# The first token loads of a 2048-token attention-plus-MLP block: two transfers of two token blocks each, one issued by SyncE and one by ScalarE

## The chip, the cores and the metric

The kernel runs on one core of a Trainium2 chip. The metric is the device time of one execution in microseconds (us). TensorE is called PE here, VectorE DVE, ScalarE ACT, GpSimd POOL and SyncE SP, as in the profile. PEld is PE's weight load.

## The reference

One pre-norm transformer block over 2048 tokens of width 640, in bfloat16: a layer norm, a linear-memory ("infini") attention with 32 heads of 20 in four segments of 512 tokens, a residual, a second layer norm, a 640-1728-640 MLP with SiLU, and a residual.

```python
q, k, v = x @ wq, x @ wk, x @ wv             # x = layernorm(A_x); 32 heads, 4 segments of 512 tokens
for s in range(4):
    p = softmax(q[s] @ k[s].T * scale + mask)            # causal inside the segment
    a_mem = (phi(q[s]) @ M) / (phi(q[s]) @ z + 1e-6)     # memory of earlier segments
    o[s] = g * a_mem + (1 - g) * (p @ v[s])              # g = sigmoid(beta), per head
    M += phi(k[s]).T @ v[s];  z += sum(phi(k[s]))
h = A_x + o @ wo
out = h + silu(layernorm(h) @ w1) @ w2
```

## The kernel before

The tokens are worked on in 16 blocks of 128 (one block is 128 partitions of 640 elements, 160 KB) and in four segments of four blocks. A segment runs through layer norm, projections, scores with exp, values, memory, output projection, second norm and MLP. The segments overlap in time.

Nothing decides an order at run time. Each step is a named task, and the text `ORDER` lists all tasks in one sequence; every engine executes its own tasks in that sequence, each instruction waiting on semaphores for what it reads. A number behind a name gives the buffer that the task takes (`x0:0` puts token block 0 into slot 0 of `x_tok`), and a letter behind a slash gives the engine where there is a choice (`A` is ACT, `D` DVE, `G` POOL). Without a letter a task goes to the first engine in its list.

The names at the start of the sequence that matter here:

- `x0`, `x1`, `x2`: loads of token blocks from `A_x` into `x_tok` (line 598, `load_x(first block, number of blocks, ..., engines)`). Before, x0 is block 0, x1 is block 1, x2 is blocks 2 and 3 in one transfer, all issued by SP. Blocks 4 to 7 (`x4`) and 8 to 11 (`x8`) come later.
- `w_q0`, `w_q1`, `w_k0`, `w_k1`, `w_wv`, `beta`: the loads of the query, key and value weights and of beta (lines 601 and 609), from SP, directly behind the token loads.
- `warm`: ACT loads its function table and runs one activation on zeros (line 618).
- `n1_st0` to `n1_st3`: mean and variance of a block. Blocks 0, 1 and 3 are done by DVE (lines 785, 788, 791), block 2 by ACT (lines 778, 780, 801).
- `n1_rs*`: reciprocal standard deviation, on POOL (line 808; 811 and 813 for block 2). `n1_ap*`: the normalised block, on DVE (line 819).
- `n1_tp*`: PE's transposition of the normalised block (line 828, five matmuls against the identity). `n1_te*`: its copy from PSUM, on ACT (line 837) or DVE (line 838).
- `fill*`: matmuls on zeros, which keep PE occupied at the start (line 637).
- `pr000x`, `pr001x`, `pr001y`, `pr000y`: the first query and key projections (line 752), from the raw weights, for blocks 0 and 1 (x) and blocks 2 and 3 (y). They are PE's first work with a result that lasts.

On DVE the sequence is statistics of block 0, statistics of block 1, normalise block 0, statistics of block 3, normalise blocks 1, 3 and 2. On PE it is transpositions of blocks 0, 1 and 3, the first part of `pr000x`, the transposition of block 2, and the rest.

Of the kernel before, what the change touches and what calls it, by code (L numbers as in the profile page):

```python
# [11 lines left out]
PE, AC, DV, PO, SP = "pe", "act", "dve", "pool", "sp"  # L12
# [368 lines left out]

ORDER = """
x0:0 zpad:0 iota fill25:7 vpad0 x1:3 sel halfc mq0 x2:5,6 warm:0 w_q0:0 epsc w_q1 n1_st0:1 w_k0:0 w_k1 w_wv:0 n1_st1:0
n1_rs0 beta n1_ap0:0 n1_rs1 fill4:5 n1_st2:5,1 n1_st3:4 fill8:5 mq1 n1_tp0:2 n1_ap1:2 n1_rs3 n1_te0:1 n1_tp1:0 n1_rs2
fill2:5 n1_ap3:3 n1_mn2 n1_te1 n1_tp3:6 n1_ap2 re_wq1/A:0 pr000x.0:3 n1_te3/D x4:2,10,11,1 n1_tp2:4 pr000x.1
x8:9,8,4,7 n1_te2 pr001x.0:1 qe000x/D:0 re_wk1/G pr001x.1 re_wk2/A pr001y.0:2 re_wk4/G pr001y.1 qe001x pr000y.0:6
# [97 lines left out]
def build(nc, es, A_x, A_wq, A_wk, A_wv, A_wo, A_beta, B_x, B_w1, B_w2, out):  # L484
# [52 lines left out]
    zpad = sb("zpad", [128, 256], BF16)  # L537
# [37 lines left out]
    def dma(name, reads, writes, fn, prio, bw, kind="plain", lane=None, engs=(SP,)):  # L575
        ln = T.lane(name) if lane is None else lane

        def emit(eng):
            T.add(eng, lambda e: fn(e), reads=R(*reads), writes=R(*writes), lane=ln)
        cost = {"tr": 1.31, "plain": 0.47, "sb": 0.72, "fix": 0.47}[kind]  # L580
        t = G.task(name, {e: cost for e in engs}, emit, reads, writes, prio, mode=kind, bw=bw)
        return t
# [12 lines left out]
    def load_x(b0, n, prio, bw=2.1, kind="plain", engs=(SP, AC)):  # L595
        s0 = b0 % 12
        dma(f"x{b0}", [(W["wk"], ["p"])] if b0 >= 4 else [], [(X[b], [0]) for b in range(b0, b0 + n)],
            lambda e: e.dma_start(out=x_tok[:, s0:s0 + n, :], in_=xv[:, b0:b0 + n, :]), prio, bw, kind, engs=engs)

    def load_w(k, dst, src, prio, bw, wr, kind="plain", engs=(SP, AC)):  # L600
        dma("w_" + k, [(W["wk"], ["p"])] if kind == "plain" else [], wr, lambda e: e.dma_start(out=dst, in_=src), prio, bw, kind, engs=engs)

    cw = lambda w: w.rearrange("(c p) e -> p c e", p=128)
    load_x(0, 1, -100, 2.30, "fix", (SP,))
    load_x(1, 1, -99, 2.33, "fix", (SP,))
    load_w("wv", wv_sb[:, :, :], cw(A_wv), -98, 4.96, [(W["wv"], [0])], "fix", (SP,))
    load_x(2, 2, -97, 4.79, "fix", (SP,))
    dma("beta", [], [(C, ["beta_bc"])],
        lambda e: e.dma_start(out=beta_bc[:, :],
                              in_=A_beta.rearrange("(o n) -> o n", o=1).to_broadcast([128, H])), -92, 4.65, "fix")  # L610
# [50 lines left out]
    sel = ident[:, :].rearrange("p (r e) -> p r e", e=32)[:, :, 0:VS]  # L661
# [695 lines left out]
def bass_sequential_preLN__memory_aug_infini_attn__dense_activation_silu__prompt_kernel(  # L1357
    nc, A_x, A_wq, A_wk, A_wv, A_wo, A_beta, B_x, B_w1, B_w2, out
):
    es = ExitStack()  # L1360
    with es:
        T, finals, _ = build(nc, es, A_x, A_wq, A_wk, A_wv, A_wo, A_beta, B_x, B_w1, B_w2, out)
        with nc.Block() as block:
            T.emit(nc, block, es, final_waits=finals)
# [28 lines left out]
```

## Time and profile before

| | |
|---|---|
| median of 3 runs | 292.54 us (292.24 to 292.88) |
| the profiled execution | 292.8 us, its span 291.1 us |
| PE busy, PEld busy | 283.0 us (97%), 156.9 us (54%) |
| DVE, ACT, POOL busy | 208.7, 224.7, 138.1 us |
| granted TensorE clock | 1.0 throughout |
| DMA queue of the kernel's transfers (q1) | 48688 packets, 24.19 MB |
| HBM | 10.41 MB read, 2.62 MB written |

The span is the time from the first to the last recorded event on the core; the rest of an execution's time lies around it. "The chain of waits" is the work that ended last, followed back step by step to what released each step; listed in order of time it gives a start, a duration and the engine with the source line. A timeline row gives the start, the duration, the engine, the line and the operation, then what was written and read, the number of instructions, and in brackets the idle time ahead of the first with what ended it. SPq is SP issuing transfers.

### The profile page before, as it was taken

The page shows a single profiled execution, that of the slowest core. Times are in us where ns is not written, and L with a number is a line of the kernel's source. Part 1 is how long each engine was busy: PE and PEld are TensorE (multiplying, and loading weights), DVE is VectorE, ACT ScalarE, POOL GpSimd, SP SyncE. Part 2 cuts the span into 40 slices and gives each one's busy share as a digit, 9 for nine tenths or more (in the row PEclk, how much of TensorE's full clock was granted, in tenths as well). Part 3 has the DMA queues.
Part 4 walks back from the last instruction along what each step waited for, and adds up shares of the span by engine and source line. Part 5 has one row for each costly group of instructions (what it writes and reads, how often), then busy time and mean ns, then how long its engine had stood idle before and what let it go on. Part 6 is the DMA issues. An engine that isn't in the chain of part 4 may idle for free.

```text
span 291.1 us, 10526 instructions
## 1 busy us (share of the span) xinstructions
PE 283.0 (97%) x4587; PEld 156.9 (54%) x4587; DVE 208.7 (72%) x435; ACT 224.7 (77%) x286; POOL 138.1 (47%) x275
## 2 busy tenths in 40 slices
PE   8999989999999999999999999999999999999995
PEld 6544434445544446566643554655565557754674
DVE  5599889769998679369979972776676659436513
ACT  4999999999999999999689989999849750024300
POOL 4686668608670766609516761638435531200000
PEclk9999999999999999999999999999999999999999
DMA  7916439854565333343551327512110031340004
GB/s 207 350 57 125 85 65 303 116 55 79 121 110 126 67 86 101 47 76 60 101 183 17 66 43 102 78 19 49 25 25 2 2 69 26 75 131 0 3 5 160
DMA packets 48734, 24.86 MB, mean 85 GB/s; under 512 B 38896, under 2 KB 47472, under 8 KB 48688
## 3 DMA queue, kind: packets, MB, share of 16 engines
q1 hardware_dynamic: 48688, 24.19, 37.9%
q8 instruction: 36, 0.59, 0.9%
q14 instruction: 10, 0.08, 0.1%
HBM read 10.41 MB, written 2.62 MB: 45 GB/s over the span
## 4 chain that ended last, share of the span: by engine, by line
PE 79%; ACT 13%; DVE 4%; DMA 2%; POOL 1%; issue 1%; SPq 0%; DVEq 0%; ACTq 0%
PE ps_all L565 41%; PE ps_all L566 23%; ACT PT L1024 9%; PE ps_all L1003 7%; PE ps_all L1059 5%; ACT PT L1020 2%; DMA x_tok<-in_A_x_dram 2%; PE ps_all L1130 1%; PE ps_all L752 1%; PE ps_all L1268 1%; ACT ex L930 1%; POOL PT L1036 1%; DVE om L1149 1%; ACT oTs L1073 1%; PE ps_all L1189 1%
## 5 line engine op out<-in xcount | busy, mean ns | idle before, releaser
L1024 ACT ACTIVATE PT<-ps_all 128x1024 bf16<-128x1024 f32 x122 | 117.9, 1030 | 7.9 <-PE ps_all L1003 6.8
L1036 POOL TENSOR_SCALAR_AFFINE_SELECT PT<-PT 128x512 bf16<-128x512 bf16 x128 | 81.6, 666 | 71.6 <-ACT PT L1024 59.5
L1281 ACT ACTIVATE th<-ps_all 128x512 f32<-128x512 f32 (+1 forms) x56 | 31.5, 591 | 30.1 <-PE ps_all L565 22.5
L1287 DVE SCALAR_TENSOR_TENSOR sT<-th,ps_all 128x512 bf16<-128x512 f32 (+1 forms) x56 | 36.2, 661 | 16.8 <-ACT th L1281 16.5
L1020 ACT ACTIVATE PT<-ps_all 128x2048 bf16<-128x2048 f32 x19 | 35.7, 1878 | 3.5 <-PE ps_all L1003 3.4
L565 PE MATMUL ps_all<-w_sb,sT 128*128 128x320 bf16 x252 | 37.0, 299 | 0.0
L565 PE MATMUL ps_all<-tT,w_sb 128*128 128x512 bf16 x151 | 36.4, 380 | 0.0
L1324 DVE SCALAR_TENSOR_TENSOR x_tok<-ps_all,x_tok 128x640 bf16<-128x640 f32 (+1 forms) x17 | 13.2, 782 | 24.5 <-PE ps_all L566 16.1
L565 PEld LDWEIGHTS ps_all<-w_sb,sT 128*128 128x128 bf16 x252 | 23.7, 98 | 11.0 <-issue 1.7
L566 PE MATMUL ps_all<-w_sb,sT 128*32 128x320 bf16 x784 | 28.8, 299 | 0.0
L785 DVE BATCH_NORM_STATS2 stt<-x_tok 128x6 f32<-128x320 bf16 x62 | 27.0, 478 | 2.0 <-DMA x_tok<-in_A_x_dram 1.9
L566 PE MATMUL ps_all<-tT,w_sb 128*32 128x512 bf16 x436 | 27.1, 380 | 0.0
L566 PEld LDWEIGHTS ps_all<-w_sb,sT 128*32 128x32 bf16 x784 | 20.1, 97 | 6.7 <-issue 0.9
L565 PEld LDWEIGHTS ps_all<-tT,w_sb 128*128 128x128 bf16 x151 | 13.6, 98 | 16.1 <-issue 1.9
L1111 POOL TENSOR_TENSOR otok<-otok,om 128x320 bf16<-128x320 bf16 x24 | 18.2, 781 | 4.2 <-DVE otok L1098 4.2
L565 PE MATMUL ps_all<-wv_sb,tT 128*128 128x320 bf16 x130 | 19.9, 300 | 0.2 <-DVE zf L677 0.2
L811 POOL TENSOR_TENSOR rst<-mvt,eps_c 128x1 f32<-128x1 f32 x29 | 5.8, 201 | 27.4 <-DVE mvt L788 27.4
L819 DVE TENSOR_SCALAR xn_rot<-x_tok,mvt,rst 128x640 bf16<-128x640 bf16 x32 | 16.7, 533 | 2.5 <-POOL rst L813 1.3
L813 POOL TENSOR_TENSOR rst<-rst,eps_c 128x1 f32<-128x1 f32 x29 | 16.4, 567 | 2.3
L1246 DVE TENSOR_TENSOR x_tok<-ps_all,x_tok 128x640 bf16<-128x640 f32 x16 | 13.0, 812 | 6.0 <-PE ps_all L565 6.0
L1059 PE MATMUL ps_all<-PT,Vx 128*32 128x512 bf16 (+3 forms) x384 | 16.9, 300 | 0.2 <-ACT PT L1024 0.2
L1098 DVE TENSOR_TENSOR otok<-ps_all,rd 128x320 bf16<-128x320 f32 x32 | 15.7, 491 | 1.1
(116 smaller groups left out, 427.8 us busy)
## 6 DMA issues: line engine op xcount, KB each, us to landing
out_dram<-x_tok SPq DMA_DIRECT2D x15, 160.0 KB, 2.0
w_sb<-in_B_w_dram SPq DMA_DIRECT2D x5, 432.0 KB, 4.6
x_tok<-in_A_x_dram SPq DMA_DIRECT2D x3, 640.0 KB, 5.1
w_sb<-in_B_w_dram SPq DMA_DIRECT2D x3, 480.0 KB, 4.1
QKV<-QK SPq DMA_DIRECT2D x12, 72.0 KB
wv_sb<-in_A_wv_dram SPq DMA_DIRECT2D x1, 800.0 KB, 8.9
wo_sb<-in_A_wo_dram SPq DMA_DIRECT2D x1, 800.0 KB, 4.8
w_sb<-in_B_w_dram SPq DMA_DIRECT2D x1, 640.0 KB, 4.7
```

The source lines that it names most:

```text
L565: return [lambda e: e.matmul(out, lhsT=lhsT, rhs=rhs, start=start, stop=stop)]
L566: return [lambda e, p=p: e.matmul(out[p:p + 32, :], lhsT=lhsT[:, p:p + 32], rhs=rhs, start=start, stop=stop, tile_position=(0, p)) for p i ...
L785: T.add(DV, lambda e, hh=hh: e.bn_stats(out=stt[:, s, 6 * hh:6 * hh + 6], in_=xb[:, 320 * hh:320 * hh + 320]), reads=R((xa, xsub)), writes ...
L819: T.add(eng, lambda e: e.tensor_scalar(out=xn_rot[:, xn.slot, :], in0=x_tok[:, b % 12, :], scalar1=mvt[:, s, 0:1], scalar2=rst[:, s, :], o ...
L1003: fns.append(lambda e, j=j, o=o, r=r, q0=q0, q1=q1, qa=qa, ka=ka: e.matmul(ps_all[:, o:o + q1 - q0], lhsT=ka[32 * r:32 * r + DH, 128 * j:1 ...
L1020: T.add(AC, lambda e: e.activation(out=o, in_=src, func=ACT.Exp, scale=SCALE), reads=[("ps", z.slot + q) for z in (a, b) for q in range(2) ...
L1024: T.add(AC, lambda e: e.activation(out=pt[:, pta.slot, q0:q0 + 2, 0:width], in_=sc3[:, b0:b0 + 2, 0:width], func=ACT.Exp, scale=SCALE), re ...
L1036: fns.append(lambda e, v=v: e.affine_select(out=v, in_=v, pattern=[[0, 4], [1, 128]], compare_op=ALU.is_ge, fill=0.0, base=0, channel_mult ...
L1059: fns.append(lambda e, j=j, r=r, h=h, pa=pa, pt=pt, co=co, q0=q0, ji=ji: e.matmul(bank(po)[32 * r:32 * r + 32, q0:hi], lhsT=vtile(vx)[:, j ...
L1111: T.add(PO, lambda e: e.tensor_tensor(out=o_dst, in0=o_dst, in1=m, op=ALU.add), reads=R((oma, WH), *osub), writes=R(*osub))
L1281: T.add(AC, lambda e: e.activation(out=th[:, tha.slot, lo:hi], in_=bank(ps)[:, lo:hi], func=ACT.Tanh, scale=0.5), reads=R((ps, [0])), writ ...
L1287: T.add(DV, lambda e: e.scalar_tensor_tensor(out=sT[:, f, lo:hi], in0=th[:, tha.slot, lo:hi], scalar=1.0, in1=bank(ps)[:, lo:hi], op0=ALU. ...
```

## The change

Token blocks 0 and 1 are loaded by one transfer of 320 KB from SP, blocks 2 and 3 by one of 320 KB from ACT, and both stand first on their engines. The task `x1` is gone. Everything else keeps its order and its engine.

```diff
 ORDER = """
-x0:0 zpad:0 iota fill25:7 vpad0 x1:3 sel halfc mq0 x2:5,6 warm:0 w_q0:0 epsc w_q1 n1_st0:1 w_k0:0 w_k1 w_wv:0 n1_st1:0
+x0:0,3 zpad:0 iota fill25:7 vpad0 sel halfc mq0 x2/A:5,6 warm:0 w_q0:0 epsc w_q1 n1_st0:1 w_k0:0 w_k1 w_wv:0 n1_st1:0
...
     cw = lambda w: w.rearrange("(c p) e -> p c e", p=128)
-    load_x(0, 1, -100, 2.30, "fix", (SP,))
-    load_x(1, 1, -99, 2.33, "fix", (SP,))
+    load_x(0, 2, -100, 2.80, "fix", (SP,))
     load_w("wv", wv_sb[:, :, :], cw(A_wv), -98, 4.96, [(W["wv"], [0])], "fix", (SP,))
-    load_x(2, 2, -97, 4.79, "fix", (SP,))
+    load_x(2, 2, -97, 4.79, "fix", (AC,))
```

The new text is one line shorter, so line numbers behind the loads are lower by one in the changed kernel.

SP at the start of the program, before the change and then with it:

```order
L598 DMA x_tok<-in_A_x_dram 128x640 x2
L598 DMA x_tok<-in_A_x_dram 128x2x640
L601 DMA sT<-in_A_wq_dram 128x3x640
L601 DMA sT<-in_A_wq_dram 128x2x640
L601 DMA sT<-in_A_wk_dram 128x3x640
```

```order
L598 DMA x_tok<-in_A_x_dram 128x2x640
L601 DMA sT<-in_A_wq_dram 128x3x640
L601 DMA sT<-in_A_wq_dram 128x2x640
L601 DMA sT<-in_A_wk_dram 128x3x640
L601 DMA sT<-in_A_wk_dram 128x2x640
```

Three transfers of tokens stood ahead of the query weights (`sT` holds the raw weights at the start); now one does, and it carries blocks 0 and 1.

ACT at the start of the program, before and then with the change:

```order
L618 ACT_TABLE_LOAD
L618 ACTIVATE w_sb<-zpad 128x1280 [waits s_dve]
L778 ACTIVATE xn_rot,stt<-x_tok 128x640 [waits l_x2]
L780 ACTIVATE xn_rot,mvt<-x_tok,stt 128x640 [waits s_act]
L837 ACTIVATE tT<-ps_all 128x5x128 [waits s_pe]
```

```order
L598 DMA x_tok<-in_A_x_dram 128x2x640
L617 ACT_TABLE_LOAD
L617 ACTIVATE w_sb<-zpad 128x1280 [waits s_dve]
L777 ACTIVATE xn_rot,stt<-x_tok 128x640 [waits l_x2]
L779 ACTIVATE xn_rot,mvt<-x_tok,stt 128x640 [waits s_act]
```

The transfer of blocks 2 and 3 now stands ahead of ACT's table load; the rest follows as before, and the statistics of block 2 still wait for that transfer (`l_x2`).

DVE from the statistics of block 0 to those of block 3, before and then with the change:

```order
L785 BN_STATS stt<-x_tok 128x6 [waits l_x0]
L788 BN_AGGR mvt<-stt 128x2 [waits s_dve]
L785 BN_STATS stt<-x_tok 128x6 [waits l_x1]
L819 TENSOR_SCALAR xn_rot<-x_tok,mvt,rst 128x640 [waits s_pool]
L785 BN_STATS stt<-x_tok 128x6 [waits l_x2]
```

```order
L784 BN_STATS stt<-x_tok 128x6 [waits l_x0]
L787 BN_AGGR mvt<-stt 128x2 [waits s_dve]
L784 BN_STATS stt<-x_tok 128x6 x2
L818 TENSOR_SCALAR xn_rot<-x_tok,mvt,rst 128x640 [waits s_pool]
L784 BN_STATS stt<-x_tok 128x6 [waits l_x2]
```

The instructions and their order stay (rows alike in both are left out). The first statistics now wait for the transfer of both blocks, and those of block 1 wait for nothing of their own.

## The prediction

> **What bounds the kernel now.** I read the chain of waits first, in order of time, to see whether the token loads stand on it at all; then DVE's and ACT's timelines at the start, to see what each load releases; then the DMA issues and the moved bytes per half microsecond, to see when the loads can land. The chain, with start, duration, engine and line:
>
> ```profile
> 0.80 0.40 SPq L598
> ...
> 1.26 0.42 SPq L598
> ...
> 1.72 4.91 DMA x_tok<-in_A_x_dram
> ...
> 6.65 0.90 DVE stt L785 x2
> ...
> 8.06 0.69 POOL rst L808
> ...
> 8.85 0.46 DVE xn_rot L819
> ...
> 9.35 0.45 PE ps_all L828 x5
> 9.80 0.47 PE ps_all L752 x12
> ...
> 10.31 0.45 PE ps_all L828 x5
> 10.77 2.07 PE ps_all L752 x68
> 12.84 0.65 PE ps_all L566 x12
> ...
> 30.66 0.36 PE ps_all L1003 x8
> ```
>
> The end of the kernel hangs on the transfer of blocks 2 and 3: it is issued third, at 1.72 us, and lands 4.91 us later, at 6.63. Then DVE takes the statistics of block 3, POOL its reciprocal, DVE normalises it, and PE transposes it at 9.35. From there to 31 us the chain stays on PE with hardly a gap. In the view of waits from 9 to 31 us PE has one:
>
> ```profile
> PE ps_all L828 <- DVE xn_rot L819: 0.3, 1, 0.3
> ```
>
> That is the wait for block 3, which ends at 9.35. Whatever this start gains or loses therefore goes through to the end, nearly whole: PE is busy 97% of the span, ACT's work from 13 us on is fed by the same matmuls, and the order on every engine is fixed. DVE and ACT at the start:
>
> ```profile
> 3.10 0.89 DVE L785 BATCH_NORM_STATS2 stt<-x_tok 128x6 f32<-128x320 bf16 x2 [1.20 <-DMA x_tok<-in_A_x_dram]
> ...
> 4.33 0.88 DVE L785 BATCH_NORM_STATS2 stt<-x_tok 128x6 f32<-128x320 bf16 x2
> ...
> 5.56 0.44 DVE L819 TENSOR_SCALAR xn_rot<-x_tok,mvt,rst 128x640 bf16<-128x640 bf16 x1
> 6.65 0.89 DVE L785 BATCH_NORM_STATS2 stt<-x_tok 128x6 f32<-128x320 bf16 x2 [0.66 <-DMA x_tok<-in_A_x_dram]
> ```
>
> ```profile
> 0.80 1.28 ACT L618 ACT_TABLE_LOAD   x1 [0.80 <-PEq L1378]
> 2.09 1.27 ACT L618 ACTIVATE w_sb<-zpad 128x1280 bf16<-128x1280 bf16 x1
> 6.65 0.74 ACT L778 ACTIVATE xn_rot<-x_tok 128x640 bf16<-128x640 bf16 x1 [3.29 <-DMA x_tok<-in_A_x_dram]
> ...
> 8.34 0.68 ACT L837 ACTIVATE tT<-ps_all 128x640 bf16<-128x640 f32 x1
> ```
>
> This is the view that decides. DVE has two waits for loads: until 3.10 for block 0, and then only **0.66 us** (6.00 to 6.65) for blocks 2 and 3, because in between it has 2.90 us of work on blocks 0 and 1 without a pause (3.10 to 5.56 + 0.44 = 6.00). So the late transfer on the chain is covered by DVE's own work but for 0.66 us. That is all that an earlier landing of blocks 2 and 3 can be worth, however early it is. ACT's 3.29 us of waiting for the same transfer is not the bound: with it gone, normalising block 3 still waits for DVE.
>
> **The change part by part.**
>
> *Blocks 2 and 3 earlier.* Their issue moves from 1.72 to about 0.80. Worth 0.66 us at most, as said; below, the landing is found early enough for all of it.
>
> *Blocks 0 and 1 in one transfer, beside another of the same size.* Now the statistics of block 0 cannot start before both blocks are there. If the pair lands at time t, DVE begins at t, works 2.90 us, and starts on block 3 at t + 2.90 where it started at 6.65. The shift of the chain is **t - 3.75 us**: a pair landing before 3.75 is a gain, after it a loss. Everything turns on t. The issues (size, median time to landing) and the bytes per half microsecond (start:end, length, clock, DMA share, GB/s):
>
> ```profile
> x_tok<-in_A_x_dram SPq DMA_DIRECT2D x2, 160.0 KB, 2.3
> x_tok<-in_A_x_dram SPq DMA_DIRECT2D x1, 320.0 KB, 4.9
> ...
> sT<-in_A_wk_dram SPq DMA_DIRECT2D x1, 320.0 KB, 7.3
> ```
>
> ```profile
> 1.50:2.00 0.50, 1.00 0.33 41
> 2.00:2.50 0.50, 1.00 0.77 236
> 2.50:3.00 0.50, 1.00 0.97 318
> 3.00:3.50 0.50, 1.00 0.95 128
> 3.50:4.00 0.50, 1.00 0.75 210
> 4.00:4.50 0.50, 1.00 0.94 330
> 4.50:5.00 0.50, 1.00 1.10 323
> 5.00:5.50 0.50, 1.00 1.02 335
> 5.50:6.00 0.50, 1.00 0.99 364
> 6.00:6.50 0.50, 1.00 1.09 376
> ```
>
> The lower bound of t with both blocks: before, block 1 was issued at 1.26 and landed 2.3 us later, 3.56, with nothing beside it but block 0. Below that, 3.1 (when block 0 alone was there) would need twice the bytes in the same time. The upper bound: a 320 KB transfer that takes 4.91 us from issue, as the one before did, lands at 0.80 + 4.91 = 5.71.
>
> Between them I choose by the bytes. Before, the two halves went one behind the other; now they start together, and the trace shows the mover as the limit, not the issuing: its DMA share is 0.75 to 1.10 from 2 us on. So I take it that the two halves share it evenly and both are complete when all four blocks are, 640 KB = 655 kB. Up to 2.5 us 0.5 x (41 + 236) = 138 kB have moved. The other 517 kB need 1.58 us at 327 GB/s (the mean of the rows 2.5 to 3.0 and 4.0 to 5.5), which ends at 4.08, or 1.38 us at the best row, 376, which ends at 3.88. From the last byte to the start of the waiting engine there is a tail: block 0's 164 kB were through at 2.5 + 25/318 = 2.58, and DVE began at 3.10, so 0.5 us. That gives t = 4.6 or 4.4, and I take **4.5**. If the weak stretch of 3.0 to 4.0 us (128 and 210 GB/s) stays, the 655 kB are through at 4.57 as before, and t is 5.1.
>
> The shift is then 4.5 - 3.75 = **+0.75 us**: the 0.66 us of waiting are gone, and the first wait has grown from 3.10 to 4.5, by 1.4.
>
> The Trainium skill speaks against this change, too. On the page DMA: Bandwidth & Descriptors, section Issuing engines are not separate DMA queues, it says that transfers started by different engines run on the same 16 DMA engines and interleave, so that a second issuer saves only the time of issuing. By that rule t is the 4.4 to 4.6 above; a second issuer with its own bandwidth would give 3.56. No run so far shows two issuers side by side.
>
> *SP's issues.* One issue fewer, and the weights behind it are issued about 0.9 us earlier. I cost this at nothing: those transfers stand in the stream of bytes, which is full from 4 us on, so an earlier issue does not land them earlier. They have to be later than they are to hurt: the last key weights land at 3.76 + 7.3 = 11.1, and PE comes to them after 20 of the 68 matmuls of the row at 10.77, at 10.77 + 20 x 2.07/68 = 11.4. So they also cap a gain: PE cannot run more than 0.3 us ahead of now unless they come earlier.
>
> *ACT's issue.* By the 0.40 us of an issue on SP, ACT's table load and warm-up end at 3.8 instead of 3.4. Both lie inside the 3.29 us in which ACT waits for the tokens, which cannot land by 3.8. Without that cover the price would be 0.4 us, on the statistics of block 2 alone. These now run at about 4.6 to 6.4, and the first copy (8.34) no longer waits behind them. Nothing gained: PE's next step needs block 3.
>
> The sum: +0.75 us, nothing else. Against the profiled execution, 292.8 us with a span of 291.1, that is 293.55. Its own time is 0.26 above the median of the three runs; on the median, 292.54 + 0.75 = **293.3 us**.
>
> **The rivals.**
>
> *Blocks 0 and 1 go ahead of blocks 2 and 3 on the movers (not slower).* If SP's rows are served first, because SP's transfer starts some tenths earlier or because the movers finish one queue's share before turning to the other, t lies between 3.56 and 4.3; at 3.8 the shift is +0.05 and the time 292.6. Blocks 2 and 3 then land where the 655 kB end, before 5.1, and DVE wants them at 6.7. It decides from t = 3.75 on. For it: the transfers are equal in size, so any lead of SP's is kept. Against it: the two issues stand at the same place of their engines, both of which begin at 0.80. The same skill page, section Queues, rings and completion order, has the engines take turns by packets of some 9 to 17 descriptors; each engine's share of a pair is 16 rows, so by it one turn could nearly be the whole pair. The time by that is this rival's.
>
> *A slow mover holds the pair (slower).* Before, the 320 KB transfer landed at 6.63, although the bytes of all four blocks were through at 4.57 in total: 2.06 us of tail instead of 0.5. Some mover was late. If this comes from the start of the two-block form and not from its place in the stream, the pair of blocks 0 and 1 has it now: t = 5.71, +1.96 us, 294.5. For it: that tail. Against it: blocks 0 and 1, in the same place of the stream, showed none.
>
> *The start of the stream is faster (faster).* With two transfers at work at once the weak stretch may vanish: (330 - 169) x 1.0 = 161 kB, half a microsecond for everything behind it, weights included, which lifts the cap of 0.3. If the pair then lands as early as block 0 did, 3.1, the shift is -0.65 and the time 291.9. Against it: twice the bytes in that time.
>
> **How the numbers follow.** What a measurement of this kernel can tell from no change is about 0.2%, 0.58 us, so slower begins at 293.12 (t = 4.33) and faster ends at 291.96. The forecast, an even share (t from 4.2 to 5.1, 293.0 to 293.9), has 0.43; the pair ahead 0.32; the slow mover 0.16; the fast start 0.09. Slower: 0.36 of the first and 0.16 of the third, 0.52. Same: 0.07 of the first, 0.29 of the second, 0.02 of the fourth, 0.38. Faster: 0.03 and 0.07, 0.10. The range reaches from 292.2 (t = 3.4) to 294.5; the forecast's own is 293.0 to 293.9.
>
> **What would show it.** In the changed kernel's DVE timeline the first statistics start at t: 4.4 to 5.1 by the forecast, 3.6 to 4.3 by the second case, over 5.5 by the third. DVE's wait for blocks 2 and 3 (0.66 us) is gone in all; if a wait stands there still, that transfer was not early, and the whole account is wrong. PE's transposition of block 3 moves from 9.35 to 10.1, and the matmul at 30.66 by as much. If the start moves by 0.75 and the end does not, later slack took it up. ACT's table load starts about 0.4 us later and delays nothing.

## The result: 0.7% slower

| | before | with the change |
|---|---|---|
| median of 3 runs | 292.54 us (292.24 to 292.88) | 294.68 us (294.54 to 295.02) |
| ratio, 95% interval | | 1.0069 [1.0048, 1.009] |
| profiled execution, span | 292.8, 291.1 us | 295.02, 293.2 us |
| mean granted TensorE clock in it | 1.0 | 0.994 |

The change costs 2.1 us, where the prediction had 0.75. The direction is right, and the time lies 0.2 us above the range. The chain of waits of the changed kernel, in order of time (start, duration, engine, line):

```profile
0.80 3.88 DMA x_tok<-in_A_x_dram
...
4.71 0.90 DVE stt L784 x2
...
7.61 0.81 DVE stt L784 x2
...
10.68 0.75 DVE xn_rot L818
...
11.47 0.71 PE ps_all L827 x5
12.19 2.93 PE ps_all L751 x63
15.12 0.65 PE ps_all L566 x11
...
32.94 0.36 PE ps_all L1002 x8
```

The chain now begins with the pair of blocks 0 and 1 and runs through DVE, as the prediction said. The matmul that stood at 30.66 us is at 32.94, 2.28 later, and the last output operation on DVE starts 2.3 us later (its group in the view of the tile `x_tok`, before and then with the change: duration in ns as min/median/max, first and last start in us, forms):

```profile
L1324 DVE SCALAR_TENSOR_TENSOR x_tok<-ps_all,x_tok x17: 491/824/826, 124.2 to 288.1; 128x640 bf16<-128x640 f32 x15, 128x320 bf16<-128x320 f32 x2
```

```profile
L1323 DVE SCALAR_TENSOR_TENSOR x_tok<-ps_all,x_tok x17: 491/824/825, 126.5 to 290.4; 128x640 bf16<-128x640 f32 x15, 128x320 bf16<-128x320 f32 x2
```

So all of the loss arises before 15.12 us, where 12.84 stood, and none of it is taken up later. The pieces stand in four views. DVE's timeline of the changed kernel (start, duration, what was written and read, in brackets the idle time ahead and its releaser):

```profile
4.71 0.89 DVE L784 BATCH_NORM_STATS2 stt<-x_tok 128x6 f32<-128x320 bf16 x2 [2.81 <-DMA x_tok<-in_A_x_dram]
...
7.52 0.88 DVE L784 BATCH_NORM_STATS2 stt<-x_tok 128x6 f32<-128x320 bf16 x2
...
9.71 0.45 DVE L818 TENSOR_SCALAR xn_rot<-x_tok,mvt,rst 128x640 bf16<-128x640 bf16 x1 [0.52 <-POOL rst L807]
10.68 0.74 DVE L818 TENSOR_SCALAR xn_rot<-x_tok,mvt,rst 128x640 bf16<-128x640 bf16 x1 [0.52 <-POOL rst L812]
```

**First piece, +0.87 us.** The pair lands at 4.69, DVE works without a pause to block 3 at 7.52 where 6.65 stood, and the wait of 0.66 us for blocks 2 and 3 is gone. This is the predicted mechanism.

**Second piece, +0.29 us.** The last row, which normalises block 2, takes 0.74 us; the same operation on block 3 in the row above takes 0.45, and before it was 0.45 for block 2 too:

```profile
9.81 0.45 DVE L819 TENSOR_SCALAR xn_rot<-x_tok,mvt,rst 128x640 bf16<-128x640 bf16 x1 [0.52 <-ACT tT L837]
```

What ran beside it is in POOL's timeline, before and then with the change:

```profile
11.20 2.62 POOL L747 COPY wkr<-sT 128x640 bf16<-128x640 bf16 x7 [1.50 <-DMA sT<-in_A_wk_dram]
```

```profile
10.52 2.66 POOL L746 COPY wkr<-sT 128x640 bf16<-128x640 bf16 x7
```

Before, POOL's copies of the key weights waited 1.50 us for a load and began at 11.20, when DVE was done with block 2 (9.81 + 0.45). Now they wait for no load and begin at 10.52, and DVE's instruction of 10.68 falls inside them.

**Third piece, +1.12 us.** The windows of the changed kernel (window, its length; PE busy and instructions, PEld, DVE, ACT, POOL the same way; granted clock, DMA share, GB/s):

```profile
7.00:8.00 1.00, 0.34 (x5) 0.28 (x5) 0.96 (x5) 0.00 (x0) 0.67 (x2) 1.00 1.08 365
8.00:9.00 1.00, 0.12 (x3) 0.00 (x0) 0.93 (x5) 0.80 (x2) 0.68 (x6) 1.00 1.07 364
9.00:10.00 1.00, 0.67 (x7) 0.39 (x7) 0.48 (x2) 0.27 (x1) 0.92 (x3) 1.00 1.07 366
10.00:11.00 1.00, 0.79 (x17) 0.56 (x17) 0.48 (x2) 1.00 (x2) 1.00 (x2) 0.86 1.07 351
11.00:12.00 1.00, 0.88 (x13) 0.45 (x5) 1.00 (x2) 0.07 (x1) 1.00 (x3) 0.50 1.10 352
...
14.00:15.00 1.00, 1.00 (x44) 0.92 (x36) 0.00 (x0) 0.61 (x2) 0.00 (x0) 0.94 0.80 261
```

From 10.7 to 14.1 us (the last 0.28 of the window at 10, the first 0.12 of the one at 14) TensorE is granted half its clock. The transposition of block 2 takes 0.71 instead of 0.45 and the first projections 2.93 instead of 2.07: 0.26 + 0.86. Ahead of it PE waits three times, for 2.4 us in all, from 7 us on; in the kernel before it waits twice in that stretch, for 0.7 us, of which the prediction, whose view begins at 9 us, quoted the wait of 0.3:

```profile
PE ps_all L827 <- DVE xn_rot L818: 2.4, 3, 1.1
```

PE was busy 1.13 of the 3 us from 7 to 10. In the kernel before it was 2.35:

```profile
7.00:8.00 1.00, 1.00 (x12) 0.78 (x10) 0.93 (x5) 0.97 (x3) 0.00 (x0) 1.00 0.91 293
8.00:9.00 1.00, 0.64 (x8) 0.39 (x7) 0.48 (x2) 1.00 (x4) 0.87 (x3) 1.00 1.05 378
9.00:10.00 1.00, 0.71 (x17) 0.51 (x17) 0.48 (x2) 1.00 (x4) 0.70 (x1) 1.00 1.05 373
```

The sum: 0.87 + 0.29 + 0.26 + 0.86 = 2.28 us, which is the shift at 15 us and at 31 us. One trace does not show that these pieces are causes, nor that they are the same in every execution. That is what the experiments are for.

### The profile page after: what moved, and what is told of

The parts are those of the page before. It is cut to its first block, busy times and chain, and to the rows that moved or that the text cites. A ratio compares the mean times of both kernels' runs of the same rounds, so it can differ in the third digit from the quotient of the medians.

```text
span 293.2 us, 10501 instructions
## 1 busy us (share of the span) xinstructions
PE 280.9 (96%) x4563; PEld 157.1 (54%) x4587; DVE 208.6 (71%) x435; ACT 225.3 (77%) x286; POOL 138.6 (47%) x275
## 4 chain that ended last, share of the span: by engine, by line
PE 78%; ACT 13%; DVE 5%; POOL 1%; DMA 1%; issue 1%; DVEq 0%; ACTq 0%; POOLq 0%
PE ps_all L565 40%; PE ps_all L566 23%; ACT PT L1023 9%; PE ps_all L1002 7%; PE ps_all L1058 5%; ACT PT L1019 2%; DMA x_tok<-in_A_x_dram 1%; PE ps_all L751 1%; PE ps_all L1129 1%; DVE stt L784 1%; PE ps_all L1267 1%; ACT ex L929 1%; POOL PT L1035 1%; DVE xn_rot L818 1%; DVE om L1148 1%
## 5 line engine op out<-in xcount | busy, mean ns | idle before, releaser
L565 PE MATMUL ps_all<-tT,w_sb 128*128 128x512 bf16 x141 | 34.5, 379 | 1.1 <-issue 0.8
```

Source lines behind the costliest of these rows:

```text
L565: return [lambda e: e.matmul(out, lhsT=lhsT, rhs=rhs, start=start, stop=stop)]
```

## The experiments

Theory A is this reading: the late pair, POOL's copies beside DVE, and a clock that falls because PE idles. Its rivals say that the late pair alone carries the loss, that ACT's queue or the larger form of the transfer does, or that the half clock is accidental. The kernel before was run beside each group, 69 times in all, with medians of 292.93, 292.95 and 292.7 us, and ratios are to these. "DVE starts" are the starts of the first statistics of block 0 and of block 3 in the run's trace; "half clock" counts the executions whose mean granted clock is 0.993 or 0.994 (3.4 us at half clock in 293 is 0.006) and not 0.998 or more.

| run | median us | ratio, 95% interval | DVE starts | half clock |
|---|---|---|---|---|
| before, all groups | 292.7 to 292.95 | | 3.10, 6.65 | 0 of 69 |
| changed kernel, first runs | 294.68 | 1.0069 [1.0048, 1.009] | 4.71, 7.52 | 1 of 3 |
| changed kernel again | 294.67 | 1.0075 [1.0046, 1.0104] | 5.02, 7.83 | 2 of 6 |
| change, more zero matmuls | 294.71 | 1.0065 [1.005, 1.008] | 4.70, 7.51 | 0 of 6 |
| change, wider zero matmuls | 294.5 | 1.0053 [1.0033, 1.0072] | 4.80, 7.61 | 0 of 8 |
| the same, POOL's copies held | 294.38 | 1.0041 [1.0025, 1.0058] | 4.88, 7.70 | 0 of 10 |
| change, fewer zero matmuls | 294.73 | 1.0067 [1.0046, 1.0087] | 4.62, 7.43 | 6 of 6 |
| before, fewer zero matmuls | 292.75 | 0.9995 [0.9981, 1.0009] | 3.12, 5.94 | 2 of 12 |
| before, pair on SP | 293.4 | 1.0014 [1.0003, 1.0025] | 3.88, 6.70 | 0 of 12 |
| before, blocks 2 and 3 on ACT | 293.08 | 1.001 [0.9998, 1.0022] | 3.21, 6.20 | 0 of 12 |
| the same, behind ACT's warm-up | 293.24 | 1.0015 [1.0, 1.0029] | 3.07, 6.67 | 0 of 12 |
| before, block 1 on ACT | 293.38 | 1.0016 [1.0002, 1.003] | 3.77, 6.58 | 0 of 12 |

### Which half of the change costs: the pair on SP, or the transfer on ACT

One part alone. In the first kernel blocks 0 and 1 come in one transfer, and blocks 2 and 3 stay behind it on SP:

```diff
-x0:0 ... x1:3 sel ...
+x0:0,3 ... sel ...
...
-    load_x(0, 1, -100, 2.30, "fix", (SP,))
-    load_x(1, 1, -99, 2.33, "fix", (SP,))
+    load_x(0, 2, -100, 2.80, "fix", (SP,))
```

> Blocks 0 and 1 in one transfer, but blocks 2 and 3 still issued by SP, right behind it. Theory A (the pair is late because blocks 2 and 3 share the movers with it): the pair lands at 3.5 to 3.7, DVE starts block 3 at 6.5 to 6.7 (whichever is later, its own work or the transfer), and the time is 292.4 to 292.7 us. Rival (a two-block transfer at the start of the stream is itself slow, whoever stands beside it): the pair lands at 4.5 or later and the time is above 293.5 us.

In the second only blocks 2 and 3 move to ACT's queue:

```diff
-... x2:5,6 ...
+... x2/A:5,6 ...
...
-    load_x(2, 2, -97, 4.79, "fix", (SP,))
+    load_x(2, 2, -97, 4.79, "fix", (AC,))
```

> Blocks 0 and 1 as before in two transfers from SP, blocks 2 and 3 in one from ACT, issued first there. Theory A (even sharing): block 0 lands near 3.6, block 1 near 4.7, DVE starts block 3 at about 6.5, the clock holds, and the time is 292.3 to 292.7 us. Rival (a transfer from ACT's queue at the start costs what was lost, whatever the order of the rest): 294 us or more.

Measured: 1.0014 [1.0003, 1.0025] and 1.001 [0.9998, 1.0022], so either half alone costs a fifth of the loss or less, and the second's interval includes no loss at all. Both times, 293.4 and 293.08 us, lie above what even sharing was expected to give and below what the rivals gave. DVE's timeline of the pair on SP, without a transfer on ACT:

```profile
3.88 0.89 DVE L784 BATCH_NORM_STATS2 stt<-x_tok 128x6 f32<-128x320 bf16 x2 [1.99 <-DMA x_tok<-in_A_x_dram]
...
6.70 0.88 DVE L784 BATCH_NORM_STATS2 stt<-x_tok 128x6 f32<-128x320 bf16 x2
```

Here, with blocks 2 and 3 behind it on SP, the pair lands at 3.86, only 0.3 us later than block 1 did as a transfer of its own (3.53). DVE needs 2.82 us from its start to block 3, so the pair may land at 6.65 - 2.82 = 3.83 without loss, and it does so within 0.05 us. In the changed kernel the same transfer, issued at the same moment, lands at 4.69. The difference, 0.8 us, is there only with ACT's transfer beside it. This trace ends 0.02 us later than that of the kernel before, so the 0.4 us of the median are not in it and stay unexplained. The issues of the second kernel, blocks 2 and 3 on ACT and block 0 and block 1 apart on SP (KB each, median us from issue to landing):

```profile
x_tok<-in_A_x_dram ACTq DMA_DIRECT2D x1, 320.0 KB, 3.4
x_tok<-in_A_x_dram SPq DMA_DIRECT2D x2, 160.0 KB, 2.8
```

Block 0 lands at 3.18 beside ACT's 320 KB, 0.1 us later than before, but block 1, second on SP, at 4.58 instead of 3.53: the load of all tokens is shared, and here the small transfer that comes first escapes it (not so below, with block 1 on ACT). DVE has block 3 at 6.20, and the matmul of 30.66 us comes 0.43 earlier, but at the end of that trace 0.15 is left (0.28 is lost near 67 us, where PE waits for the transposed tiles `sT<-otok`), and the median is not better. So most of the loss needs both halves together: two transfers of 320 KB that start side by side, with DVE waiting for all of one.

### Does the transfer on ACT do less harm when it starts later

The kernel before, with blocks 2 and 3 on ACT behind its table load and warm-up in the order:

```diff
-... x2:5,6 warm:0 w_q0:0 ...
+... warm:0 x2/A:5,6 w_q0:0 ...
...
-    load_x(2, 2, -97, 4.79, "fix", (SP,))
+    load_x(2, 2, -97, 4.79, "fix", (AC,))
```

> The kernel before with only blocks 2 and 3 moved to ACT's queue, behind ACT's table load and warm-up instead of ahead of them, so that blocks 0 and 1 have the movers to themselves at the start. Block 0 lands at 3.1 and block 1 at 3.5 as before; blocks 2 and 3, issued at 3.4, land at 5.7 to 6.2; DVE starts block 3 at 6.0 to 6.2 instead of 6.65, and the shift at 14 us is -0.4 to -0.6. Of the gain about half was lost later where ACT issued first (there -0.43 at 14 us and -0.15 at the end); so 0.1 to 0.5 us below the kernel before. If blocks 2 and 3 land after 6.7, as slow as before, no gain.

Its premise fell: ACT's queue issued the transfer at 1.11 us, in the midst of the table load that stands ahead of it in the program. ACT's rows of this run:

```profile
0.80 1.28 ACT L618 ACT_TABLE_LOAD   x1 [0.80 <-PEq L1378]
1.11 0.47 ACTq L598 DMA_DIRECT2D x_tok<-in_A_x_dram  x1
```

So the two loads ran side by side again, and DVE had to wait for block 1:

```profile
5.08 0.89 DVE L785 BATCH_NORM_STATS2 stt<-x_tok 128x6 f32<-128x320 bf16 x2 [0.69 <-DMA x_tok<-in_A_x_dram]
```

Block 3 at 6.67, as before; 293.24 us, 1.0015 [1.0, 1.0029], and none of the gain of 0.1 to 0.5 us that was expected. In this trace, too, the weights came early and block 2's normalising fell beside POOL's copies: it took 0.99 us, and the shift at 14 us is +0.56. A later start of blocks 2 and 3 was thus not tried.

Another way to divide the load, only block 1 on ACT:

```diff
-... x1:3 ...
+... x1/A:3 ...
...
-    load_x(1, 1, -99, 2.33, "fix", (SP,))
+    load_x(1, 1, -99, 2.33, "fix", (AC,))
```

> The kernel before with only block 1 moved to ACT's queue, first there; SP has block 0 and then blocks 2 and 3. By even sharing of the movers blocks 0 and 1 land together at 3.2 to 3.6, blocks 2 and 3 at 4.6 to 5.5; DVE starts block 3 at 6.1 to 6.5 (its own work from the landing on, 2.9 us) and waits for nothing, so 0.1 to 0.5 us earlier than in the trace of the kernel before. Of that at most half reaches the end, by the earlier runs: 292.6 to 293.0 us beside a kernel before of about 292.9. If blocks 2 and 3 land after 6.7 there is no gain.

Both land together, block 0 at 3.75 and block 1 at 3.57, and block 3 starts at 6.58, 0.07 earlier than before: 293.38 us, 1.0016 [1.0002, 1.003], no gain, where 292.6 to 293.0 was expected. Here two transfers of half the size, started together, land 0.2 us or less apart: even sharing again, and the one that DVE needs first pays. Block 0 lands 0.7 us later than in the kernel before, although ACT's transfer beside it is half as large as the one beside which it lost 0.1; so what a small first transfer loses is not settled by one trace of each.

### How the landing of the pair varies, and what the loss is with the clock held

The changed kernel was run again without an edit.

> The changed kernel once more, unaltered, for a second trace and for times beside the two below. Its first trace had DVE's start on block 3 0.87 us late, block 2's normalising 0.3 us longer beside POOL's copy, and PE at half clock from 10.7 to 14.1 us, in all 2.28 us at 13 us and the same 2.29 at the end. Theory A (three terms, as said): 2.0 to 2.3 us over the kernel before, and the first projections (68 matmuls) again take about 3.0 us instead of 2.1. Theory B (the half clock was an accident of that one execution): the projections take 2.1 us, the shift at 14 us is 1.2, and something later must make up the rest.

294.67 us, 1.0075 [1.0046, 1.0104]. The executions fall in two: 294.36, 294.4, 294.46 and 294.89 at full clock, 296.16 and 296.32 with the half-clock stretch. The profile caught one of the first, and its chain reads:

```profile
12.23 2.07 PE ps_all L751 x68
14.30 0.65 PE ps_all L566 x12
```

The projections take 2.07, as before the change, and yet the chain is 1.46 us late at 14.30 and 1.48 at the end. DVE's timeline has the cause:

```profile
5.02 0.89 DVE L784 BATCH_NORM_STATS2 stt<-x_tok 128x6 f32<-128x320 bf16 x2 [3.12 <-DMA x_tok<-in_A_x_dram]
...
7.83 0.88 DVE L784 BATCH_NORM_STATS2 stt<-x_tok 128x6 f32<-128x320 bf16 x2
...
10.98 0.74 DVE L818 TENSOR_SCALAR xn_rot<-x_tok,mvt,rst 128x640 bf16<-128x640 bf16 x1 [0.52 <-POOL rst L812]
```

The pair landed at 4.99 this time, so block 3 is 1.18 later, and the normalising of block 2 takes 0.74 again: 1.18 + 0.29 = 1.47. The four executions at full clock have a median of 294.43, 1.48 above the 292.95 of the kernel before in that group: trace and time agree. The half clock is thus no part of every execution of the change, and the loss stands without it.

The kernel before, one more look:

> The kernel before once more, unaltered, for a second trace. Its first had blocks 2 and 3 landing at 6.63 and DVE's start on block 3 at 6.65; with 12 fill matmuls fewer and the same loads they landed at 5.92 and DVE waited for nothing. If this landing varies by that much between executions, the kernel before itself varies by about 0.6 us at the start, and the 0.66 us of waiting in its first trace was a bad case: I expect a landing between 5.5 and 6.7 and a start on block 3 between 6.0 and 6.7.

293.7 us, with blocks 2 and 3 landing at 6.59 and DVE's wait for them 0.67: the late landing on which the prediction built is there again. In the run with fewer zero matmuls, which has the same loads, they landed at 5.92 and DVE did not wait. So the wait that the change removes is there in two of three traces. These traces also show how much two executions of the same order differ later on: the second of the kernel before is 0.04 us ahead of the first at 31 us and 0.33 behind it at the end.

### Does idle time of PE bring the half clock, and what does the half clock cost

PE is kept busy at the start by zero matmuls (the `fill` tasks). Two kernels give PE more of this work, and two take some away. The change with 20 more:

```diff
-... fill4:5 n1_st2:5,1 n1_st3:4 fill8:5 mq1 n1_tp0:2 n1_ap1:2 ...
+... fill4:5 n1_st2:5,1 n1_st3:4 fill18:5 mq1 n1_tp0:2 fill8:5 n1_ap1:2 ...
-fill2:5 n1_ap3:3 ...
+fill4:5 n1_ap3:3 ...
```

> The changed kernel with 20 more matmuls on zeros on PE (10 before the transposition of block 0, 8 between blocks 0 and 1, 2 more before block 3), nothing else. Theory A (the 2.1 us are three terms: DVE starts block 3 0.87 us later because the pair lands at 4.69; block 2's normalising takes 0.3 us longer beside POOL's copy; and PE's idle time of 2.4 us lets its clock fall to one half around 11 to 14 us, which costs 1.1 us): DVE's start on block 3 stays near 7.5, the clock stays at 1.0, the first projections take 2.1 us again instead of 3.0, and the time is 293.5 us. Theory B (all of it is the late landing and slower work behind it, the clock is a side effect without a price): 294.7 us as without the fill.

The clock held in all six, and in the trace the first projections took 2.07 and the shift at 31 us was 1.14, half of the 2.28. But the median did not move: 294.71, what theory B had for it and not theory A's 293.5. From 31 us on this trace loses what it had won and ends 2.2 us late. Part of it shows as waits of PE's loads between 235 and 262 us:

```profile
PEld ps_all L565 <- DMA tT<-otok: 0.9, 2, 0.6
PEld ps_all L565 <- DMA tT<-xn_rot: 0.5, 1, 0.5
```

In the same stretch of the kernel before, PE's loads waited for no transfer. Why they come is not known; 20 more instructions on PE are one difference. To leave that out, the next kernel keeps the number of zero matmuls and makes 14 of them twice as wide (512 columns):

```diff
-... fill25:7 vpad0 ...
-n1_rs0 ... fill4:5 n1_st2:5,1 n1_st3:4 fill8:5 mq1 n1_tp0:2 n1_ap1:2 ...
-fill2:5 n1_ap3:3 ...
+... fill21:7 vpad0 ...
+n1_rs0 ... fill4:5 n1_st2:5,1 n1_st3:4 fill8/W:5 mq1 n1_tp0:2 fill4/W:5 n1_ap1:2 ...
+fill2/W:5 n1_ap3:3 ...
...
```

(The lines left out give `fill` its width.)

> The changed kernel with as many matmuls on zeros as before (39), but 14 of them 512 columns wide instead of 256, and four of these moved between the transpositions of blocks 0 and 1; no instruction is added on any engine, so the run with 20 more matmuls is repeated without its longer program. Theory A: the clock holds, the shift at 14 us is 1.2 us, and the time is 1.0 to 1.3 us over the kernel before. Theory B: 2.0 us or more over it, as without the fill and as with the 20 more.

The clock held in all eight; 294.5 us, 1.0053 [1.0033, 1.0072], 1.55 above the kernel before, between theory A's 1.0 to 1.3 and theory B's 2.0. In the window from 7 to 10 us PE is busy 2.30 of 3 us against 1.13 in the changed kernel, and DVE 2.38 as there:

```profile
7.00:10.00 3.00, 2.30 (x18) 0.98 (x16) 2.38 (x9) 0.97 (x3) 2.18 (x8) 1.00 1.07 365
```

The shift at 14 us is 1.25, the late pair and POOL's copies, 0.96 + 0.29; at the end it is 1.42. Now fewer. The kernel before without the groups of 4 and of 8:

```diff
-... fill4:5 n1_st2:5,1 n1_st3:4 fill8:5 mq1 ...
+... n1_st2:5,1 n1_st3:4 mq1 ...
```

> The kernel before, with 12 of its 39 matmuls on zeros taken out (fill4 and fill8), so that PE idles ahead of the first transpositions with the loads untouched. Theory A: the clock falls to one half within a few us of the idle time, and the time rises by 0.8 to 1.3 us, to about 293.6, with DVE's start on block 3 still near 6.65. Theory B: no effect, 292.5 us, as nothing waits for these matmuls.

292.75 us, 0.9995 [0.9981, 1.0009]: no difference, which theory A had not expected. The half clock came in 2 of 12, at 293.42 and 293.79; the trace is of one without it, with PE busy 1.98 of the 3 us. And the change without the same two groups:

> The changed kernel with 12 of its 39 matmuls on zeros taken out (fill4 and fill8), so that PE idles about 1.3 us more ahead of the first transposition; the suspected cause of the half clock is enlarged. So far the half clock (a mean clock of 0.994) came in 3 of 9 executions of the changed kernel, in 2 of 12 of the kernel before with the same 12 taken out, in none of 24 with wider or more fill. Theory A: it comes in most executions, the median is 1.0 to 1.8 us over the changed kernel's, near 296 us. Theory B (its coming has nothing to do with PE's idle time): in a third of them at most, median near 294.7 us.

Here the half clock came in 6 of 6. The windows (as above):

```profile
6.00:7.00 1.00, 0.13 (x2) 0.00 (x0) 0.94 (x3) 0.74 (x2) 0.56 (x1) 1.00 1.08 366
7.00:8.00 1.00, 0.42 (x5) 0.28 (x5) 0.99 (x4) 0.00 (x0) 0.76 (x2) 1.00 1.07 360
8.00:9.00 1.00, 0.03 (x1) 0.00 (x0) 0.93 (x4) 0.79 (x2) 0.68 (x5) 0.94 1.08 366
9.00:10.00 1.00, 0.85 (x7) 0.67 (x7) 0.48 (x2) 0.09 (x1) 0.92 (x3) 0.50 1.06 362
...
12.00:13.00 1.00, 1.00 (x31) 0.64 (x28) 0.39 (x2) 0.72 (x2) 1.00 (x4) 0.86 1.07 374
```

PE was busy 0.58 of 3 us, and the clock fell earlier, from 8.9 to 12.3. That is under PE's waits for DVE, where a slower PE delays little: the transposition of block 2 still takes 0.71 instead of 0.45, but the projections take 2.14 in all. Of the shift of 1.47 at 14 us, 0.78 is block 3 (7.43), 0.29 the copies, and 0.40 at most is left for the clock; at the end the shift is 1.86. The median is 294.73, not the 296 that theory A had for it. So the two sides of theory A part: **that idle time of PE brings the half clock is shown by its frequency**. Where PE was busy for 19% of 3 us (here, from 6 to 9 us; in all others from 7 to 10) it came in 6 of 6, at 38 to 42% in 3 of 9, at 57 to 66% in 2 of 36 (the pair on SP and block 1 on ACT, 0 of 12 each, and the kernel before with fewer zero matmuls), and at 77% or more in 0 of 117 (all the rest). Each share is that of one or two traces of the kernel. **What it costs depends on which work falls into the 3.4 us**, from 0.4 us at most at 14 us here to the 1.12 us of the first profiled execution.

The traces also show what decides within one kernel. The changes of the clock lie whole steps of 3.413 us apart: in this run it falls at 8.87, rises at 12.29 and falls again behind the last matmul at 292.18, 82 steps later. In the step ahead of a fall PE was busy 1.12 of 3.41 us here (5.46 to 8.87, 33%) and 1.62 in the first profiled execution (7.30 to 10.71, 48%). In the repeated execution of the change, counted back from its fall behind the last matmul at 292.04, the steps from 5.32 and from 8.73 have PE busy for 2.50 and 1.93 us (73 and 57%), and the clock held. So the same waits can be split over two steps or fill one, and the border, by these three traces, lies between 48 and 57% of a step. That is an inference from two falls; no run varied where the steps begin.

The Trainium skill, TensorE: Matmul & The Clock Gate, section Part 1: The HAM clock gate, describes two speeds, full and half, set by the activity in windows of about 3.4 us whose start the kernel doesn't choose. The traces agree: each stretch is 3.4 us at 0.50 (10.72 to 14.12, and 8.88 to 12.28 here), and at 38 to 42% of activity it comes in some executions and not in others. That section has the clock fall after an idle window of that length; here it fell with no wait of PE over 1.13 us ahead of it in the changed kernel, and with PE busy for 48% of the step, so a window without work is not needed for it.

### Is it POOL's copy that lengthens DVE's instruction

The kernel with the wider zero matmuls, and one tiny write on POOL that waits for the normalising of block 2 and stands ahead of the copies (it writes a constant that holds the same value already):

```diff
+        if tag == "n1_" and b == 2:
...
+                e_plain(eng)
+                T.add(PO, lambda e: e.memset(eps_c[:, 0:1], EPS), reads=R((xn, [0])), writes=R((C, ["eps"])))
```

> The same with one POOL instruction more (a memset of one column ahead of POOL's weight copies) that waits until block 2 is normalised, so that the copies no longer run beside it. If POOL's copy is what made that DVE instruction 0.75 us instead of 0.45, it takes 0.45 again, the shift at 14 us is 0.85 to 0.9, and the time is 0.3 us below the run with wide fill alone. Rival (the longer normalising has another cause, the transfers for instance): still 0.75 us, and no gain, or a loss through POOL's later copies.

POOL's and DVE's timeline of this run:

```profile
10.85 0.45 DVE L818 TENSOR_SCALAR xn_rot<-x_tok,mvt,rst 128x640 bf16<-128x640 bf16 x1 [0.52 <-POOL rst L812]
11.35 0.10 POOL L827 MEMSET eps_c<- 128x1 f32 x1 [0.62 <-DVE xn_rot L818]
11.45 1.64 POOL L746 COPY wkr<-sT 128x640 bf16<-128x640 bf16 x4
```

With the copies behind it, the instruction takes 0.45 again instead of 0.74, and the shift at 14 us is 1.04, the lateness of block 3 alone (7.70 - 6.65 = 1.05). So POOL's copies are the cause of the second piece, 0.29 us, in the trace. The median shows less of it: 294.38 us, 1.0041 [1.0025, 1.0058], is the lowest of the changed kernels, but only 0.12 below its neighbour, where 0.3 was expected, and the intervals overlap. At the end of this trace the shift is 1.30. The Trainium skill has this on the page SBUF — State Buffer, section Who interferes with whom: while VectorE's fast form of such an instruction runs, it and GpSimd shut each other out. The durations agree that DVE is held up: 0.45 alone, and 0.74 or 0.99 beside copies that take 2.66 / 7 = 0.38 each.

## Why the prediction was half right

**What was right.**

- *The chain hangs on the token loads and the shift is t - 3.75.* Right in form. DVE begins when the pair is there and reaches block 3 2.81 to 2.82 us later in all six traces of the changed loads, not 2.90, so the constant is 3.84.
- *The wait for blocks 2 and 3 is worth 0.66 us and no more.* Nearly right: it is gone in all six. By DVE's 2.81 us it was worth 6.65 - (3.10 + 2.81) = 0.74, and in the run with fewer zero matmuls, where it is gone with the loads untouched, block 3 starts at 5.94.
- *The two queues share the movers evenly.* Right as against the second case, the pair ahead: with SP alone it lands at 3.86, beside ACT's transfer at 4.60 to 4.99, and ACT's transfer lands 0.3 to 0.4 us behind it in all six traces (5.05 against 4.69 in the first). Moving blocks 2 and 3 to ACT without pairing delays block 1 in the same way.
- *Whatever the start loses goes through to the end.* Right for the loss: 2.28 at 15 and at 31 us, 2.3 at the end. For gains it was not: 0.43 at 31 us became 0.15 with blocks 2 and 3 alone on ACT, and 0.64 became 0.28 with fewer zero matmuls.
- *ACT's issue is hidden.* Right: the table load starts at 1.31 instead of 0.80 in the changed kernel, and nothing waits for it.

**What was wrong.** The step that failed is "The sum: +0.75 us, nothing else". Three terms:

- *t was taken as 4.5 and is 4.60 to 4.99* (six traces; DVE starts at 4.62 to 5.02, 4.79 on average). The weak stretch of 3 to 4 us was gone, as the rival of the faster stream had it, but both transfers start slowly, which the working had not in it. Bytes of the changed kernel, per half microsecond (window, length, clock, DMA share, GB/s):

```profile
1.50:2.00 0.50, 1.00 0.27 28
2.00:2.50 0.50, 1.00 0.76 138
2.50:3.00 0.50, 1.00 0.87 256
3.00:3.50 0.50, 1.00 0.85 248
```

By 2.5 us 0.5 x (28 + 138) = 83 kB had moved, where the prediction took over 138 from the rows of before. The 55 kB that are missing are 0.17 us at 327 GB/s, by this estimate about the miss in this trace (4.69 against 4.5). On the average of the six traces this term is 0.95 us (4.79 - 3.84), and 0.87 in the first profiled execution.

- *"An earlier issue does not land them earlier"* was wrong here. The last key weights, issued 0.88 us earlier, land at 9.54 instead of 11.06, and their copies on POOL no longer wait 1.50 us for them. The issue alone does not do it: with the pair on SP these weights are issued 0.36 us earlier and land at 11.19; with only blocks 2 and 3 on ACT they land at 10.28. Beside two transfers at once the stream was ahead: by 6.5 us the rows of the changed kernel add up to 1483 kB against 1330. This earlier landing hurts, since DVE is late at the same time: POOL starts its copies at 10.52 beside DVE's normalising of block 2, **+0.29 us**. The prediction looked at the weights only as a cap on a gain and left out who else is set free by them.
- *No term for PE.* The prediction followed what PE waits for and not what waiting does to PE's clock. The half clock comes in 3 of 9 executions and cost **1.12 us** in the profiled one.

For the median the account is 0.95 for the pair and 0.29 for the copies, 1.24, and in some executions the half clock. At full clock the repeated runs show 1.48, and so does their one trace, in which the pair landed late (1.18 + 0.29). With the clock held by wider fill the median is 1.55 above the kernel before, and 1.43 with the copies held too, where the account has 1.24 and 0.95: it falls short by 0.2 to 0.5 us. The first three runs show more, +2.1, partly since the median of three of the kernel before, 292.54, is 0.2 to 0.4 below the medians of 17 to 29 of its runs.

**The rivals.** The slow mover had the right time, 294.5, by a way that did not happen: the pair lands at 4.60 to 4.99 and not at 5.71. The fast start was right on the stream and wrong on what it would bring.

**What stays open.** Single traces lose up to 0.4 us behind 31 us, and the one with 20 more zero matmuls 1.1 (PE waits for transposed tiles, near 67 us in one and between 235 and 262 us in another), and no run tells why. The 0.2 to 0.5 us by which the account falls short may be of this kind; that is not shown. The half clock's price by the executions is 0.4 us in the first three runs (295.02 against 294.54 and 294.68), 1.8 in the repeated ones (296.24 against 294.43), and 1.1 in the kernel before with fewer zero matmuls (293.42 and 293.79 against a median of 292.52 for the other ten), with 1.12 in the one trace; no trace was kept of the last four, so whether more than the stretch differs in them is not known. With both later terms held away, the changed kernel is still at 1.0041 [1.0025, 1.0058], and of the 1.30 us by which its trace ends late, 1.04 are the late pair: that alone makes it slower. No version of the study is faster than the kernel before.

## What to carry to other kernels

When two loads are put on two queues, ask which bytes the first consumer waits for: started together they share the movers, and the first consumer then waits for nearly the sum of both. Serving it a small load first and the rest behind costs nothing as long as its work on the first covers the landing of the rest; here that cover was 2.8 us, and all that was to be won behind it was the one wait of 0.66, which one trace of the same loads did not even have. And price an earlier landing both ways: what it sets free may run into the instruction on the chain, and a longer wait of PE may cost its clock as well as the wait.

## What the runs showed of the hardware that was not expected

- A transfer that stands behind a table load in ACT's program was issued at 1.11 us, while the table load ran from 0.80 to 2.08. ACT's queue does not hold a transfer until the instruction ahead of it is done.
- The clock fell to half for 3.41 us after a stretch of the same length in which PE had been busy 48% in the changed kernel, with no wait of PE over 1.13 us; in another execution of the same kernel it held at 57%. In the kernel before, with PE busy 78% of 7 to 10 us in one trace and 88% in the other, it fell in none of 69 executions.
- Two transfers of 320 KB started together by SP and ACT land 3.8 to 4.5 us after issue, where one with the next behind it on its own queue needs 3.1 (0.80 to 3.86). One of 160 KB beside one of 320 KB landed only 0.1 us later than without it, in the one trace of this, but 0.7 later beside one of 160 KB.
- The landing of the same 320 KB transfer, third on SP, was 6.63, 6.59 and 5.92 us in three traces of the same loads.
